# Pairs of row quadrants in one PSUM tile, and a written order for the tensor engine, in a decode-attention and MLP backward kernel

## The chip, the cores and the metric

The kernel runs on one core of a Trainium2 chip. The metric is device time in microseconds, from repeated executions; lower is better. Executions of one kernel here differ by one to two per cent, so each changed version is compared with executions of the kernel before on the same chip in the same rounds. A ratio is the mean time of one kernel's fast runs over that of the other's of the same rounds, so it isn't quite the ratio of the medians that are quoted. A run counts as slow, and is left out of a ratio, when it is over 1.5% above the fastest of its kernel. Spans and shares are from one profiled execution.

PE is the tensor engine (PEld its weight loads), DVE the vector engine, ACT the scalar engine, POOL the engine that issues the output DMAs, SP the queue that issues the loads. PSUM is the memory in which matmuls leave their results; an eviction is the copy of such a tile to SBUF, from where it is stored. A row quadrant is 32 of the 128 rows of PE's array (32*128 in the profile's forms, where the full array is 128*128). The granted clock is the share of its full speed that PE's clock has, by the records of the profile.

## The reference, cut to what matters

One decode step (2 rows, one token each) of attention with a long cache plus a gated MLP, and the gradients of all of it:

```python
B, D, Hq, Hkv, Sk, Dh, F = 2, 576, 32, 16, 4096, 128, 4608     # bf16
def fwd(x, k_cache, v_cache, wq, wo, w_gate, w_up, w_down):
    xn = layernorm(x)
    q = heads(xn @ wq)
    p = softmax(einsum("bhqd,bhkd->bhqk", q, repeat(k_cache)) * Dh ** -0.5)
    o = einsum("bhqk,bhkd->bhqd", p, repeat(v_cache))
    h = (xn @ w_gate) * (xn @ w_up)
    return x + merge(o) @ wo + h @ w_down
out, vjp = jax.vjp(fwd, ...)
return (out, *vjp(grad_out))       # also dk_cache, dv_cache, and every weight's gradient
```

dk_cache and dv_cache are as large as the caches, 92 MB in and 92 MB out in all. Each is a set of outer products: a column of probabilities (or of their gradients) times a row of 128.

## The kernel before: the parts that matter

There are eight iterations: four groups of four kv heads, times two batch rows. In an iteration the four K heads are loaded, transposed on DVE and scored, then there is a softmax, the four V heads are scored for the gradient of the probabilities, and two contracts (probabilities with V, score gradients with K) follow. Outer products (`outs`) and slices of the MLP and projections (`side`) are popped in between by `fill`.

```python
def ps_o():                                    # two buffers of [128, 2 banks, 512] fp32
    return ps.tile([P, 2, 512], FP32, tag="o", bufs=2, name="ps_o")

def head_scores(src, t, b, g, l, s_ps):
    n = nat([P, NCH, Dh], "kv")                # one of 11 buffers
    nc.sync.dma_start(...)                     # 1 MB
    X = xtile(...);  t32(X, n)                 # 32x32 transposes on DVE, one of 2 buffers
    for be in range(4):
        for cq in range(4):
            nc.tensor.matmul(s_ps[:], lhsT=..., rhs=view(X[:], ...))       # 128x128 array, 256 columns
    return n

def unit(A, cq):                               # of outer_units
    o = [ps_o(), ps_o()]
    for h in range(2):
        for aa in range(2):
            a = 2 * A + aa                     # row quadrant of the array, 32 rows
            nc.tensor.matmul(o[aa][:, h, :], lhsT=rows[32 * a:32 * a + 32, P * h:P * (h + 1)],
                             rhs=BD[t][32 * a:32 * a + 32, cq, :], start=True, stop=True)
    for aa in range(2):
        evac(..., o[aa][:]...)                 # to SBUF on ACT or DVE, 1024 columns

for n in range(NIT):
    ...
    for l in range(G):
        K.append(head_scores(kview, 0, b, g, l, s_ps))
        fill(2, per)                           # two outer units and `per` side units
    ...
    pr, pT, ex, rz = softmax(s_ps)
    ...
    for l in range(G):
        V.append(head_scores(vview, 1, b, g, l, dp_ps))
        if l > 0: contract(pT, V[l - 1], o_sb, l - 1)
        fill(2, per)
    ...                                        # end of V, then the contract of K in the same iteration
```

The order in which PE issues is not the written one here. A scheduler at build time reorders the instructions of each engine.

## Time and profile before

| | before |
|---|---|
| two timed runs | 680.32 and 682.2 us, median 681.26 |
| span of the profiled execution | 666.9 us |
| PE busy | 574.7 us, 86% |
| PE idle between its first and last matmul (gaps over 0.06 us) | 72.8 us |
| mean granted PE clock over the span | 0.716 |

How to read it: PE is nearly always occupied, and its clock stands at full or half speed in turn (the trace's 46 clock records are all 1.0 or 0.5, and each but the last lasts a multiple of 3.413 us; mean 0.716). The prediction shows the main lines. The longest waits of PE (what it waited for, microseconds in total, times, longest):

```profile
PE ps_m L488 <- ACT o_sb L491: 11.4, 3, 4.9
PE ps_m L184 <- DVE xn_bf L165: 10.7, 1, 10.7
PE ps_o L512 <- ACT so L93: 7.9, 27, 1.2
PE ps_sc L475 <- DVE negb L540: 7.7, 4, 2.1
```

No group of waits costs PE more than 11.4 us in the whole program: nearly every hand-over has other work behind it.

### The profile page before, as it was taken

The page shows a single profiled execution, that of the slowest core. Times are in us where ns is not written, and L with a number is a line of the kernel's source. Part 1 is how long each engine was busy: PE and PEld are TensorE (multiplying, and loading weights), DVE is VectorE, ACT ScalarE, POOL GpSimd, SP SyncE. Part 2 cuts the span into 40 slices and gives each one's busy share as a digit, 9 for nine tenths or more (in the row PEclk, how much of TensorE's full clock was granted, in tenths as well). Part 3 has the DMA queues.
Part 4 walks back from the last instruction along what each step waited for, and adds up shares of the span by engine and source line. Part 5 has one row for each costly group of instructions (what it writes and reads, how often), then busy time and mean ns, then how long its engine had stood idle before and what let it go on. Part 6 is the DMA issues. An engine that isn't in the chain of part 4 may idle for free.

```text
span 666.9 us, 14489 instructions
## 1 busy us (share of the span) xinstructions
PE 574.7 (86%) x6297; PEld 298.5 (45%) x6297; DVE 360.4 (54%) x499; ACT 330.7 (50%) x445; POOL 129.8 (19%) x252
## 2 busy tenths in 40 slices
PE   1679997897989999897999999899796999989954
PEld 1455553545534445444543454355553345453411
DVE  8686245546594246636484345637287134862245
ACT  0145655283555545374445635456362655645441
POOL 6131201131121121221122221112022111201111
PEclk9998868597886558598776557578597556885555
DMA  8965989559959879749949969829977688834355
GB/s 296 373 234 189 364 325 371 185 178 420 393 201 340 325 246 339 291 154 408 388 163 365 321 249 348 312 83 362 403 280 267 228 295 326 305 133 166 128 197 197
DMA packets 52824, 185.89 MB, mean 279 GB/s; under 512 B 4077, under 2 KB 19065, under 8 KB 44569
## 3 DMA queue, kind: packets, MB, share of 16 engines
q1 hardware_dynamic: 28392, 92.49, 38.4%
q0 software_dynamic: 24368, 92.48, 37.4%
q8 instruction: 49, 0.80, 0.5%
q14 instruction: 15, 0.11, 0.1%
HBM read 92.48 MB, written 92.48 MB: 277 GB/s over the span
## 4 chain that ended last, share of the span: by engine, by line
PE 49%; issue 15%; DMA 10%; ACT 9%; DVE 8%; POOL 1%; ACTq 0%; POOLq 0%; DVEq 0%
PE ps_o L512 16%; PE ps_sc L475 14%; DMA out_dram<-so 10%; ACT so L93 7%; PE ps_m L488 5%; DVE X L102 3%; PE ps_m L497 2%; PE ps_o L379 2%; PE ps_o L345 2%; DVE so L90 1%; PE ps_m L253 1%; PE ps_m L417 1%; DVE Xw L102 1%; PE ps_o L655 1%; DVE stq L90 1%
## 5 line engine op out<-in xcount | busy, mean ns | idle before, releaser
L93 ACT CAST so<-ps_o 128x1024 bf16<-128x1024 f32 x222 | 217.1, 1019 | 174.2 <-PE ps_o L512 116.7
L475 PE MATMUL ps_sc<-X,W 128*128 128x256 bf16 x1024 | 189.7, 328 | 13.2 <-DVE negb L540 7.7
L102 DVE STREAM_TRANSPOSE X<-kv 128x2048 f32<-128x2048 f32 x64 | 147.0, 2299 | 47.0 <-PE ps_sc L475 21.1
L475 PEld LDWEIGHTS <-W 128*128 128x128 bf16 x1024 | 103.9, 113 | 82.8 <-issue 55.2
L512 PE MATMUL ps_o<-BD,pr 32*128 32x512 bf16 x256 | 91.6, 488 | 6.2 <-ACT so L93 4.4
L512 PE MATMUL ps_o<-BD,ds 32*128 32x512 bf16 x256 | 81.7, 487 | 12.0 <-ACT so L93 3.5
L519 POOL DMA_DIRECT2D out_dram<-so x64 | 48.9, 765 | 193.9 <-ACT so L93 91.8
L90 DVE CAST so<-ps_o 128x1024 bf16<-128x1024 f32 x34 | 41.4, 1218 | 49.1 <-PE ps_o L512 43.3
L488 PE MATMUL ps_m<-kv,dsT 128*32 128x128 bf16 x1024 | 29.4, 285 | 11.4 <-ACT o_sb L491 11.4
L93 ACT CAST stw<-ps_o 128x1024 bf16<-128x1024 f32 x33 | 32.6, 1017 | 11.6 <-PE ps_o L345 9.7
L488 PE MATMUL ps_m<-kv,pT 128*32 128x128 bf16 x1024 | 38.2, 257 | 0.1
L488 PEld LDWEIGHTS <-pT 128*32 128x32 bf16 x1024 | 20.3, 107 | 36.1 <-issue 33.5
L488 PEld LDWEIGHTS <-dsT 128*32 128x32 bf16 x1024 | 23.1, 128 | 29.3 <-issue 27.7
L512 PEld LDWEIGHTS <-ds 32*128 32x128 bf16 x256 | 14.7, 96 | 37.3 <-issue 32.0
L497 PEld LDWEIGHTS ps_m<-R,o_sb 128*128 128x128 f32 x128 | 25.7, 281 | 11.0 <-issue 5.7
L93 ACT CAST std<-ps_o 128x576 bf16<-128x576 f32 x33 | 20.7, 640 | 18.8 <-PE ps_o L379 14.4
L497 PE MATMUL ps_m<-R,o_sb 128*128 128x2 f32 x128 | 27.7, 321 | 2.6 <-DVE cr L566 2.6
L512 PEld LDWEIGHTS <-pr 32*128 32x128 bf16 x256 | 15.7, 97 | 25.3 <-issue 16.9
L491 ACT COPY o_sb<-ps_m 128x128 f32<-128x128 f32 x64 | 17.0, 278 | 20.1 <-PE ps_m L488 19.8
L458 ACT CAST bd<-ps_m 128x512 bf16<-128x512 f32 x16 | 9.4, 587 | 30.7 <-PE ps_m L456 30.6
L379 PE MATMUL ps_o<-dyr,hb 32*128 32x288 bf16 x72 | 19.3, 365 | 4.8 <-ACT std L93 4.7
L261 DVE TENSOR_TENSOR accx<-accx,ps_m 128x160 f32<-128x160 f32 x13 | 4.0, 309 | 35.9 <-PE ps_m L258 35.9
(180 smaller groups left out, 578.4 us busy)
## 6 DMA issues: line engine op xcount, KB each, us to landing
out_dram<-so POOLq DMA_DIRECT2D x64, 1024.0 KB, 7.5
kv<-in_A_k_cache_dram SPq DMA_DIRECT2D x32, 1024.0 KB, 8.4
kv<-in_A_v_cache_dram SPq DMA_DIRECT2D x32, 1024.0 KB, 8.8
out_dram<-stw POOLq DMA_DIRECT2D x18, 512.0 KB, 8.1
wd<-in_B_w_down_dram SPq DMA_DIRECT2D x9, 576.0 KB, 8.2
out_dram<-std POOLq DMA_DIRECT2D x9, 576.0 KB, 4.4
wo<-in_A_wo_dram SPq DMA_DIRECT2D x4, 1152.0 KB, 9.4
wgu<-in_B_w_gate_dram SPq DMA_DIRECT2D x9, 512.0 KB, 9.9
```

The lines of the kernel that those rows point to most:

```text
L90: nc.vector.tensor_copy(out=out, in_=in_)
L93: nc.scalar.copy(out, in_)
L102: nc.vector.transpose(out, in_)
L345: nc.tensor.matmul(o[a // 2][:, a % 2, dc * P:(dc + 1) * P], lhsT=xnr[32 * a:32 * a + 32, dc * P:(dc + 1) * P], rhs=hb[32 * a:32 * a + 32, ...
L379: nc.tensor.matmul(o[aa][:, k, 0:HD2], lhsT=hb[32 * a:32 * a + 32, 0, :], rhs=dyr[32 * a:32 * a + 32, k * HD2:(k + 1) * HD2], start=True, ...
L458: nc.scalar.copy(bd[:], bp[:].rearrange("p l d -> p (l d)"))
L475: nc.tensor.matmul(s_ps[:], lhsT=view(W[t][:], 0, P, (be * G + l) * WW + 24 - 8 * cq, [[1, P]]), rhs=view(X[:], 0, P, 2 * cq * Dh + 64 * ( ...
L488: nc.tensor.matmul(o_ps[32 * cq:32 * cq + 32, :], lhsT=rowsT[:, 4 * h + c4, :], rhs=head[:, 8 * c4 + 2 * cq + h, :], start=(h == 0 and c4 ...
L491: nc.scalar.copy(o_sb[:, l, :], o_ps[:])
L497: nc.tensor.matmul(t_ps[:, 2 * l:2 * l + 2], lhsT=o_sb[:, l, :], rhs=R40[:, 2 * l:2 * l + 2], start=True, stop=True)
L512: nc.tensor.matmul(o[aa][:, h, :], lhsT=rows[32 * a:32 * a + 32, P * h:P * (h + 1)], rhs=BD[t][32 * a:32 * a + 32, cq, :], start=True, sto ...
L519: nc.gpsimd.dma_start(oview[b, 2 * A + aa, :, G * g:G * g + G], m["st"][aa][:].rearrange("p l c d -> p l (c d)"))
```

## The change

The intent has two parts. First, an outer product's PSUM tile is given to a pair of row quadrants, one bank each, so its two matmuls run side by side, and a tile that comes free is refilled by one such pair. Second, PE issues everything in the order of the text. That order is written so that half of a head's scores alternates with two pairs. To make it hold, loads and the build of operands move: the loads of a new group's weights, the contract of K (now in the next iteration), and the buffers (kv 11 to 10, staging 4 to 2 plus 2).

```diff
-        def unit(A, cq):
+        def unit(A, cq, h):
-                o = [ps_o(), ps_o()]
-                for h in range(2):
-                    for aa in range(2):
-                        a = 2 * A + aa
-                        nc.tensor.matmul(o[aa][:, h, :], ...)
+                o = ps_o()
                 for aa in range(2):
-                    evac(m["st"][aa]..., o[aa][:]..., 1024)
+                    a = 2 * A + aa
+                    nc.tensor.matmul(o[:, aa, :], ...)
+                evac(m["st"][:, :, :, 2 * cq + h, :], o[:]..., 1024)
  ... the same for the outer products of the MLP and of wq, wo
+    def slot(src, t, b, g, l, s_ps, per, mid=None):
+        n, X = head_load(src, b, g, l)
+        head_scores(X, t, l, s_ps, 0)       # 8 of the 16 score matmuls
+        more(2)                             # two pairs
+        head_scores(X, t, l, s_ps, 1)
+        if mid: mid()                       # a contract
+        more(2)
+        other(per)                          # side units
+        return n
+    chain = ctx.enter_context(tc.manual_schedule(engines={mybir.EngineType.PE}))
  ... in the loop:
-            K.append(head_scores(kview, 0, b, g, l, s_ps))
-            fill(2, per)
+            K.append(slot(kview, 0, b, g, l, s_ps, per, (lambda: end_of_K(*last)) if l == 0 and last else None))
+        if n + 1 < NIT and b == 1:
+            loaded = group_loads(g + 1)     # new wq and wo, while the old ones are held
-            V.append(head_scores(vview, 1, b, g, l, dp_ps))
+            V.append(slot(vview, 1, b, g, l, dp_ps, per, ...))
-        for l in range(G):
-            contract(dsT, K[l], o_sb, l)    # moved into end_of_K of the next iteration
+        last = (st, b, K, dsT)
```

## The prediction

> **What bounds the kernel now.** I read the busy table first, then the costliest groups, then the order of time on PE, the idle time of DVE, and a table by iteration.
>
> ```profile
> PE 574.7 (86%) x6297; PEld 298.5 (45%) x6297; DVE 360.4 (54%) x499; ACT 330.7 (50%) x445; POOL 129.8 (19%) x252
> L93 ACT CAST so<-ps_o 128x1024 bf16<-128x1024 f32 x222 | 217.1, 1019 | 174.2 <-PE ps_o L512 116.7
> L475 PE MATMUL ps_sc<-X,W 128*128 128x256 bf16 x1024 | 189.7, 328 | 13.2 <-DVE negb L540 7.7
> ```
>
> PE is occupied 86% of the span and nothing else is over 54%. The evictions of the outer products (L93) wait for PE 116.7 us, and the scores (L475) hardly wait for anybody. So PE is the engine to shorten, and the question is what its 575 us are made of. The timeline of PE shows two losses:
>
> ```profile
> 356.74 0.60 PE L512 MATMUL ps_o<-BD,pr 32*128 32x512 bf16 x4
> 358.48 0.59 PE L512 MATMUL ps_o<-BD,pr 32*128 32x512 bf16 x2 [0.59 <-ACT so L93]
> ...
> 331.27 0.40 PE L475 MATMUL ps_sc<-X,W 128*128 128x256 bf16 x2
> 331.60 0.41 PE L655 MATMUL ps_o<-dyr,R 32*128 32x288 bf16 x2
> 331.95 0.95 PE L475 MATMUL ps_sc<-X,W 128*128 128x256 bf16 x7
> ```
>
> Four outer products take 0.60 us, and two take 0.59. The four are two pairs from different row quadrants, which run together. The two share a quadrant and run one after the other: each PSUM tile holds one quadrant, so when one tile comes free the scheduler issues its two matmuls alone. The last three lines show PE alternating between the full array (128*128) and row tiles (32*128). From 331.27 to 331.60 are 0.33 us for two score matmuls that take 0.11 each in a run, so a change of tile shape costs about 0.11 us.
>
> The third loss is the clock. By iteration (from one softmax to the next) the view of windows gives:
>
> ```profile
> core 0: us, PE busy (x) PEld busy (x) DVE busy (x) ACT busy (x) POOL busy (x), PEclk, DMA share, GB/s
> 118.20:187.50 69.30, 61.87 (x766) 35.99 (x765) 37.74 (x51) 35.56 (x51) 14.44 (x32) 0.78 0.79 299
> 187.50:270.10 82.60, 78.57 (x764) 36.21 (x763) 45.17 (x58) 45.94 (x60) 14.21 (x25) 0.66 0.82 290
> 581.10:666.90 85.80, 63.66 (x602) 27.98 (x601) 39.34 (x60) 36.24 (x47) 14.07 (x21) 0.56 0.45 165
> ```
>
> Seven iterations lie between 45.0 and 581.1 us, 76.6 us each. The head before the first softmax is 45, the end after the last 86. In the slower iterations the granted clock is lower. DMA is busy 0.8, so loads aren't free either. The idle time of DVE shows where a load already binds:
>
> ```profile
> 144.05 2.31 DVE L102 STREAM_TRANSPOSE X<-kv 128x2048 f32<-128x2048 f32 x1 [6.67 <-DMA kv<-in_A_v_cache_dram]
> DMA to landing us min/median/max: 5.0/8.6/15.0
> ```
>
> The second line is from the view of the tile kv: a head of 1 MB lands 5.0 us after its issue at the least.
>
> [...] The trace's clock is half or full in multiples of 3.413 us. I weighted each matmul's columns by the share of the array that it uses, by window: over 2,900 of such full-array columns the next window is at full clock, under it at half, in 181 of 185 windows. [...]
>
> **The change part by part.** The work is the same (6205 matmuls in both built programs); order and buffers move.
>
> 1. Pairs. I counted the columns that the longest quadrant streams in each stretch of row-tiled matmuls: 263 thousand before, 157 thousand after. 179 of the 512 matmuls of L512 directly follow one of their own quadrant, after none does. A 512-column matmul streams in 0.215 us at full clock (two of them start 0.215 apart), 0.42 ns a column, 0.59 at the mean granted 0.716. 106 thousand columns save 62 us, 7.8 an iteration.
> 2. Changes of tile shape in PE's order: 748 before, 382 after. 366 x 0.11 = 40 us, 5 an iteration.
> 3. Evictions: as many, 227 so-evictions on ACT against 222, the same widths. Nothing saved; ACT still needs 40 us an iteration, under PE.
> 4. Clock. Full-array work is fixed, about 490 thousand columns, 61 thousand an iteration; at 76.6 us (22.4 windows) that is 2,730 a window, just below the threshold. Half a head and two pairs at half clock take 8 x 0.213 + 2 x 0.43 + 2 x 0.11 = 2.8 us for 2,560 columns, 3,100 a window: enough to lift the clock. I take 0.80 instead of 0.716.
>
> PE's own time in an iteration, before: 663 thousand streamed columns / 8 x 0.42 / 0.716 = 48.6, shape changes 10.3, the fp32 ends of contracts (L497, 1.87 us each, two) 3.7, two-column matmuls 2.3: 64.9, so 11.7 us are waits and small matmuls. After: 557 thousand / 8 x 0.42 / 0.80 = 36.5 + 5.3 + 3.7 + 2.3 = 47.8.
>
> 5. Waits that the written order adds. Before, PE did outer products meanwhile. Per iteration: the softmax, three tiny matmuls with DVE and ACT between (0.28, 0.2, 0.16, 0.5 + 0.2 us and hand-overs, sometimes a transpose of 2.3 ahead), 3.5 us; the MLP slice's chain between down and grads (0.42 + 0.4 us and a transpose of 2.5 on DVE), 3; the end of K behind ACT's copies, 1.5; BD, dscores, group front, 1.5; DVE evictions behind transposes, 3: 12.5 us.
> 6. Loads. The kv buffers go from 11 to 10, and K's four heads are held into the next iteration, until its first score head. In the built program, in every second iteration (new wq and wo are held beside the old), the load of V's third head waits for the first's contract, with only two pairs before its scores. It then takes 5.2 to land + 2.3 transpose + 0.4 = 7.9 us, of which PE covers 1. The same for V's fourth (covered 5), the next K's first (4.5), and the second, behind another load (11 against 3.5): 6.9 + 2.9 + 3.4 + 7.5 = 21 us, 10 an iteration.
>
> Sum: 47.8 + 12.5 + 10 + 3 for the small rest = 73.3 against 76.6. Head 47 (the first scores now come after more loads). End: the V half stays, the tail's pairs alternate between ACT and DVE without half-filled tiles; 79 against 86. 47 + 7 x 73.3 + 79 = 639 us in the profile, against 667. The timed runs of before are 1.02 of the profiled one: 651. I lower it to 640, because waits of 5 and 6 partly overlap each other and are counted in full.
>
> **Rivals.**
> - The loads take the place of what PE saves. For it: DMA share 0.8 before, a wait of 6.67 us already there with 11 buffers, and the waits of step 6 in the program. [...] Iterations of 80 to 85 us, 690 to 715.
> - The clock stays up. For it: every stretch of alternating halves is over the threshold[...]. [...] Then streaming is 29 instead of 36.5 and an iteration about 66 us: 590; with smaller waits 575.
> - ACT becomes the bound: 16 pairs in four heads need 4 x 1.02 us a head, PE at full clock about 5.7 with all else. For it 116.7 us of waiting turn round; against, ACT at 40 us an iteration is under any PE estimate. It would cap the gain near 590 too.
> - Saved PE time is hidden anyway: not likely, since PE sits on half of the ending chain.
>
> **Range and chances.** The central sum lies 4 to 6% below before. The added waits are the least certain term (22 us an iteration, perhaps 12 to 32, which is 70 us either way), the clock the next (7 us an iteration, 50 us). Together 80% of outcomes lie between 575 and 700. Faster by over 2% (below 667.6): 0.66. Within: 0.20. Slower: 0.14.
>
> **What would show it.** Right: two outer products of L512 in about 0.38 us at full clock, never 0.59; PE's groups by L512's line busy a third less; ACT's wait for PE on so well below 117; fewer issue gaps at weight loads; granted clock about 0.80. DVE waiting on kv loads grows from 26 us to over 50, mostly in every second iteration at V's third and fourth heads and the next K's second; PE waits on DVE's softmax results rise from about 11 us. Wrong: a clock at or under 0.72 (step 4), kv waits under 30 us (step 6), or PE idle by less than 12 us an iteration (steps 5 and 6 together).

The sum comes to 639 us in the profile, 651 in timed runs, lowered to 640. A window is a stretch of 3.413 us, and the threshold is the 2,900 full-array columns in the trace of before. Steps 5 and 6 assume that in a written order PE does nothing else during a wait. That was not shown when they were written; the runs below measure what the order costs (PE idles 213.4 us with it, 109.6 in a_sched without).

## The result, and the profile after

The changed kernel takes **746.46 us** (two runs, 742.93 and 749.99) against 681.26. The ratio is 1.1018, 95% interval 1.0843 to 1.1193: slower by a tenth. The outputs are correct.

The busy table and the two groups that the prediction started from, after (a group's line gives busy time and mean ns of one, then the idle time of its engine ahead of it and what ended it):

```profile
PE 513.3 (69%) x6297; PEld 287.7 (38%) x6297; DVE 369.7 (49%) x499; ACT 329.6 (44%) x445; POOL 130.1 (17%) x256
L93 ACT CAST so<-ps_o 128x1024 bf16<-128x1024 f32 x227 | 219.7, 1016 | 237.5 <-PE ps_o L520 215.7
L485 PE MATMUL ps_sc<-X,W 128*128 128x256 bf16 x1024 | 213.6, 377 | 68.7 <-DVE X L102 68.7
```

PE is busy 61 us less, and still the span is 81 us longer, because PE stands idle for 213.4 us instead of 72.8. ACT's waiting for PE was to shrink; it nearly doubled. The scores are as many, but take 377 ns each instead of 328, and they now wait 68.7 us for transposed heads.

The table by iteration, from one softmax to the next (columns as in the prediction's table):

```profile
59.30:135.80 76.50, 55.24 (x745) 32.16 (x741) 36.16 (x46) 40.31 (x56) 10.01 (x20) 0.75 0.73 269
135.80:233.90 98.10, 66.75 (x755) 35.22 (x753) 39.61 (x52) 42.00 (x56) 15.54 (x34) 0.62 0.61 223
233.90:314.50 80.60, 60.37 (x773) 35.31 (x771) 42.71 (x53) 40.12 (x55) 13.42 (x25) 0.71 0.81 296
314.50:413.70 99.20, 64.97 (x757) 34.86 (x754) 42.08 (x54) 39.46 (x54) 15.44 (x33) 0.65 0.61 220
669.90:748.20 78.30, 53.50 (x601) 26.94 (x600) 42.37 (x63) 36.46 (x49) 15.39 (x23) 0.61 0.52 188
```

The seven iterations take (669.9 - 59.3) / 7 = 87.2 us on average, against 76.6 before. Every second one takes some 20 us more: it holds the V half of a group's second row and the K half of the next group, with new weights loaded in it. The DMA share is lower there on average (0.61) than in the other iterations of the table (0.73 and 0.81), so these waits don't come of bandwidth alone: loads are issued late. Yet where PE waits the DMA engines are nearly full. The head that PE waits for until 202.30 (below) was issued at 192.71, while a contract still ran, and its transpose starts 7.2 us later, with the DMA share at 0.92 in that stretch. How a wait divides between the two was not measured.

PE's waits, in the same view as above for before:

```profile
PE ps_sc L485 <- DVE X L102: 68.7, 13, 9.0
PE ps_m L320 <- DVE gT L102: 26.8, 8, 4.8
PE ps_m L184 <- DVE xn_bf L165: 13.3, 1, 13.3
PE ps_o L382 <- ACT so L93: 12.2, 21, 0.9
PE ps_m L544 <- DVE mr L542: 11.8, 8, 4.5
PE ps_o L349 <- ACT so L93: 7.7, 11, 1.1
PE ps_m L551 <- ACT ex L549: 6.8, 8, 0.8
```

L485 are the scores, L320 is a middle step of the MLP chain, L544 and L551 are in the softmax. L382 and L349 are outer products of the side units, which stand in a row, two (L382) or eight (L349) matmuls to a tile, with only two tiles. Added over all their lines and releasers, the side units' outer products wait 62 us.

What the waits do to the clock is seen in PE's order of time around the start of a new group's K heads:

```profile
190.34 1.32 PE L485 MATMUL ps_sc<-X,W 128*128 128x256 bf16 x8
191.59 2.08 PE L497 MATMUL ps_m<-kv,dsT 128*32 128x128 bf16 x128
...
195.80 0.40 PE L463 MATMUL ps_m<-ident,dM 128*128 128x128 bf16 x4
202.30 1.86 PE L485 MATMUL ps_sc<-X,W 128*128 128x256 bf16 x8 [6.10 <-DVE X L102]
204.09 1.03 PE L520 MATMUL ps_o<-BD,ds 32*128 32x512 bf16 x4
205.06 1.89 PE L485 MATMUL ps_sc<-X,W 128*128 128x256 bf16 x8
```

and in the table of windows of the same stretch (window, its length, PE busy and count, granted clock, DMA share, GB/s):

```profile
188.00:195.00 7.00, 7.00 (x159) 0.79 0.32 99
195.00:202.00 7.00, 1.20 (x46) 0.70 0.92 321
202.00:209.00 7.00, 6.70 (x64) 0.50 1.01 410
209.00:216.00 7.00, 6.33 (x92) 0.50 0.79 326
```

In this trace the clock follows what PE did just before: the prediction's count (over or under 2,900 full-array columns in a window of 3.413 us) foretells full or half clock in the next window in 194 of 207. From 188 to 195 PE is busy for all 7.00 us; over the following 7 us the granted clock is 0.70 on average, and PE has only 1.20 us of work in them. When the head at last arrives at 202.3, the clock is down to 0.50, and eight scores take 1.86 us (1.32 at 190.34, where the clock changed midway). The full clock falls in the wait and the half clock on the work. The time average of the clock hides this: it is 0.703, near the 0.716 of before.

I therefore cut PE's busy intervals by the records of the granted clock. "Work" is the busy time at full clock plus half of that at half clock; "clock over work" is work over busy time. PE's busy time ahead of the first clock record is left out (11.0 us before, 12.4 after, between 5.5 and 14.6 in the other runs), so differences of some 10 us of work between runs mean little. Idle time is that between the first record and the last matmul.

| | before | after |
|---|---|---|
| PE busy at full / half clock, us | 218.8 / 344.9 | 157.8 / 343.1 |
| work, us of full clock | 391.3 | 329.3 |
| clock over work | 0.694 | 0.657 |
| idle at full clock / half clock, us | 40.6 / 25.3 | 105.0 / 96.9 |
| score matmuls issued at half clock | 39% | 74% |

The change did take 62 us of full-clock work off PE. But 105.0 us of full clock ran out while PE had nothing to do.

### The profile page after: what moved, and what is told of

Read it like the earlier page. It is cut to its first block, busy times and chain, and to the rows that moved or that the text cites. A ratio compares the mean times of both kernels' runs of the same rounds, so it can differ in the third digit from the quotient of the medians.

```text
span 748.2 us, 14452 instructions
## 1 busy us (share of the span) xinstructions
PE 513.3 (69%) x6297; PEld 287.7 (38%) x6297; DVE 369.7 (49%) x499; ACT 329.6 (44%) x445; POOL 130.1 (17%) x256
## 5 line engine op out<-in xcount | busy, mean ns | idle before, releaser
L93 ACT CAST so<-ps_o 128x1024 bf16<-128x1024 f32 x227 | 219.7, 1016 | 237.5 <-PE ps_o L520 215.7
L485 PE MATMUL ps_sc<-X,W 128*128 128x256 bf16 x1024 | 213.6, 377 | 68.7 <-DVE X L102 68.7
L485 PEld LDWEIGHTS <-W 128*128 128x128 bf16 x1024 | 123.6, 129 | 163.6 <-issue 118.6
L520 PE MATMUL ps_o<-BD,ds 32*128 32x512 bf16 x256 | 59.6, 540 | 5.2 <-ACT so L93 2.9
L520 PE MATMUL ps_o<-BD,pr 32*128 32x512 bf16 x256 | 52.7, 492 | 5.5 <-DVE so L90 2.5
L349 PE MATMUL ps_o<-hb,xnr 32*128 32x128 bf16 x288 | 17.0, 249 | 16.0 <-ACT so L93 7.7
L102 DVE STREAM_TRANSPOSE Xw<-wgu 128x2304 f32<-128x2304 f32 x9 | 23.1, 2563 | 9.7 <-PE ps_sc L485 9.7
L468 DVE TENSOR_SCALAR BD<-bd,maskc 128x512 bf16<-128x512 bf16 x64 | 19.3, 365 | 14.8 <-ACT bd L465 14.8
L497 PE MATMUL ps_m<-kv,pT 128*32 128x128 bf16 x1024 | 24.7, 251 | 0.0
L520 PEld LDWEIGHTS <-ds 32*128 32x128 bf16 x256 | 10.1, 101 | 31.3 <-issue 30.9
L497 PE MATMUL ps_m<-kv,dsT 128*32 128x128 bf16 x1024 | 19.4, 238 | 3.8 <-issue 3.8
L382 PE MATMUL ps_o<-dyr,hb 32*128 32x288 bf16 x72 | 11.5, 317 | 14.3 <-ACT so L93 12.2
L349 PEld LDWEIGHTS <-xnr 32*128 32x128 bf16 x288 | 10.9, 104 | 25.9 <-issue 25.5
```

What stands on the lines that cost most here:

```text
L93: nc.scalar.copy(out, in_)
L102: nc.vector.transpose(out, in_)
L349: nc.tensor.matmul(o[:, aa, dc * P:(dc + 1) * P], lhsT=xnr[32 * a:32 * a + 32, dc * P:(dc + 1) * P], rhs=hb[32 * a:32 * a + 32, 1 + w, :], ...
L382: nc.tensor.matmul(o[:, aa, 0:HD2], lhsT=hb[32 * a:32 * a + 32, 0, :], rhs=dyr[32 * a:32 * a + 32, k * HD2:(k + 1) * HD2], start=True, sto ...
L468: nc.vector.tensor_scalar(BD[t][:, c, :], bd[:], maskc[:, c:c + 1], None, op0=ALU.mult)
L485: nc.tensor.matmul(s_ps[:], lhsT=view(W[t][:], 0, P, (be * G + l) * WW + 24 - 8 * cq, [[1, P]]), rhs=view(X[:], 0, P, 2 * cq * Dh + 64 * ( ...
```

## The experiments

The first theory: the pairs save PE time, and the written order loses more, because each wait that is no longer filled costs its own length and lowers the clock for what comes after it. The rivals: the loads and the lost kv buffer make the whole loss (the first rival of the prediction); pairs of quadrants don't pay at all; the halves that alternate are at fault.

Eleven kernels ran. Each ratio is against the kernel before in the same rounds. Differences in us from the changed kernel (746.46) go across rounds, in which the median of the kernel before lay between 672.4 and 681.3; taken by the ratios, the changed kernel comes out 5 to 8 us nearer to the others that are faster, and as much farther from the slower ones (w_reuse 61 us less than it, w_softmax 24, w_both 86, a_sched 121; w_whole 39 more). The sign `+` or `-` in the short diffs is against the kernel that is named.

### Taking the change apart: four runs beside the same runs of the kernel before (median 672.51)

**a_sched**, the changed kernel with the scheduler free for PE:

```diff
-    chain = ctx.enter_context(tc.manual_schedule(engines={mybir.EngineType.PE}))
```

> The changed kernel without the line that fixes PE's order; all tiles, buffers and the order of the text stay. Theory W (the loss is PE waiting at the head of a fixed order): a scheduler fills the waits again, PE idles about as in the kernel before, and the pairs' saving shows: 640 to 680 us. Theory L (the loss is in the loads: ten kv buffers and K's heads held into the next iteration): the waits on kv loads stay, over 60 us by DVE, and the time stays over 715 us. In the built program the tile shape changes 656 times, and 8 matmuls follow one of their own quadrant.

Measured: 619.79 us (614.4 to 621.17), ratio 0.9212 (0.914 to 0.9284), correct, and better than the 640 to 680 that I expected. The one line costs 746 - 620 = 127 us. From its page:

```profile
PE 490.6 (79%) x6297; PEld 284.9 (46%) x6297; DVE 361.3 (58%) x499; ACT 327.4 (53%) x445; POOL 131.6 (21%) x256
L485 PE MATMUL ps_sc<-X,W 128*128 128x256 bf16 x1024 | 186.5, 328 | 34.8 <-DVE X L102 32.8
```

and from its view of DVE's waits:

```profile
DVE X L102 <- DMA kv<-in_A_k_cache_dram: 45.2, 10, 7.5
DVE X L102 <- DMA kv<-in_A_v_cache_dram: 29.2, 9, 7.8
```

The same two waits of DVE in the changed kernel:

```profile
DVE X L102 <- DMA kv<-in_A_k_cache_dram: 33.9, 10, 8.7
DVE X L102 <- DMA kv<-in_A_v_cache_dram: 32.8, 10, 9.7
```

The loads come no earlier with the scheduler free: DVE waits for them 74.4 us here and 66.7 in the changed kernel. PE merely has other work meanwhile, and so scores wait 34.8 us instead of 68.7. The scores take 328 ns again. So late loads alone are not the cause; what they cost depends on whether PE's order is fixed (PE idles 213.4 us with it fixed, 109.6 here).

**b_order**, the kernel before with PE's order fixed as written:

```diff
+    chain = ctx.enter_context(tc.manual_schedule(engines={mybir.EngineType.PE}))
     side = []
```

> The kernel before with PE's order fixed as written and nothing else changed: 11 kv buffers, K's contracts at the end of their own iteration, tiles of one quadrant. The built order changes tile shape 279 times and has no matmul that follows one of its own quadrant in the stretch's longest queue (154 thousand columns), so PE's own work is as short as in the changed kernel. Theory W: slower than before all the same, 730 to 800 us. Theory L: 630 to 690 us.

Measured: 837.46 us (832.55 to 840.29), ratio 1.246 (1.2367 to 1.2552), correct, and slower than the 730 to 800 expected. In its view of PE's waits, one stands out:

```profile
PE ps_o L512 <- ACT so L93: 96.7, 121, 1.1
PE ps_m L538 <- DVE mr L536: 19.7, 8, 3.7
```

Eight outer products stand in a row after each head there, with two PSUM tiles to take them, so PE waits for an eviction 121 times. PE's idle time rises from 73 to 243 us, which is the whole loss of 171 us between the profiled spans (666.9 to 838.5). The work falls to 332.9 us, but the clock over work falls too, to 0.596, so PE is busy as long as ever (572.4 against 574.7).

**b_pairs**, the kernel before, its loop and its free scheduler, with the paired tiles and the changed buffers:

```diff
-        def unit(A, cq):
+        def unit(A, cq, h):
-                o = [ps_o(), ps_o()]
+                o = ps_o()
   ... as in the change; fill() pops two pairs for one old unit; slot(), end_of_K and the written order left out
```

> The kernel before with only the tiles changed to pairs of quadrants (and the buffers that they need: ten kv buffers, two large staging tiles, two for the rest); its own order of the text, the scheduler free. Same-quadrant followers fall from 244 to 7, columns from 263 to 177 thousand, shape changes stay (720). Theory W: the pairs' saving shows, 86 thousand columns at 0.59 ns are 50 us of PE, so 630 to 670 us. Theory L: ten buffers cost it, 690 us or more.

Measured: 633.76 us (624.91 to 639.19). No interval was formed, as two of its four runs were over 1.5% above its fastest. The means of the fast runs give 628.1 / 671.7 = 0.935, and even its slowest run, 639.19, lies under the fastest of the kernel before, 667.24. The work falls from 391.3 to 348.2 us with as many changes of tile shape (720 against 748), and PE still has only 87.5 us of idle. So pairs pay by themselves.

**b_nat10**, the kernel before with 10 kv buffers:

```diff
-    sb.tile(..., tag="nat", bufs=11, ...)
+    sb.tile(..., tag="nat", bufs=10, ...)
```

> The kernel before with ten kv buffers instead of eleven, nothing else. Theory W: within 3% of before, 675 to 700 us. Theory L: one buffer less already costs a good part of the 65 us, 705 us or more.

Measured: 674.88 us, ratio 1.0074 (0.9983 to 1.0165). The lost buffer alone costs nothing that can be told.

### Which waits: four runs in the written order (before: median 675.41)

**w_reuse** takes the load out of the group boundary: a new group uses the old wq and wo tiles again. Its outputs are wrong.

```diff
-            loaded = group_loads(g + 1)
+            loaded = (st["wq"], st["wo"])
```

> The changed kernel, but a new group takes the wq and wo tiles of the first group again instead of loading its own (the results are wrong on purpose). The two kv buffers that the old pair held stay free, so the loads of V's third and fourth heads and of the next K no longer wait for a contract, and 6.5 MB are not read. If step 6 of the prediction is right (21 us a group boundary, 62 in all), about 680 to 700 us, scores wait for their transposes under 30 us instead of 68.7. If the loads only fill time that PE would lose to the written order anyway: over 725 us.

Measured: 677.63 us, ratio 1.011 (0.9986 to 1.0235), 69 us under the changed kernel and no longer to be told from the kernel before. The run takes out the transfers of new weights, the two buffers that they hold and the wait for them all at once, so it doesn't tell these apart. From its page:

```profile
L485 PE MATMUL ps_sc<-X,W 128*128 128x256 bf16 x1024 | 198.2, 357 | 5.0 <-DVE X L102 5.0
```

The scores' wait goes from 68.7 to 5.0 us, but PE's idle falls by only 39 us (213.4 to 174.4), as other waits take part of its place (the one at L463 grows from 6 to 21). Between the profiled spans the gain is 748.2 - 675.4 = 72.8 us. The other 31 us are busy time: 513.3 falls to 482.3, with the work not less (340.1 against 329.3; 346.8 against 341.7 with the time ahead of the records counted at full clock), since the clock over work rises from 0.657 to 0.715.

**w_softmax** puts the two score halves of the first V head between the softmax's three small matmuls:

```diff
-        pr, pT, ex, rz = softmax(s_ps)
+        one()                                 # max, transpose
   ...
+                head_scores(Xv, 1, l, dp_ps, 0)
+                two()                         # max to all rows, exp
+                more(2)
+                head_scores(Xv, 1, l, dp_ps, 1)
+                pr, pT, ex, rz = three()      # sum, divide
```

> The changed kernel in its written order, but the softmax's three small matmuls stand apart: the second behind the first half of V's first head, the third behind the second half. The 19.6 us that PE idles before them should go: 720 to 730 us. If the clock then stays up longer, less; if V's first half now waits for its transpose instead, 740 us or more.

Measured: 717.11 us, ratio 1.067 (1.0576 to 1.0764), 29 us under the changed kernel. Idle falls by 16.0 us and busy time by 14.2, at the same work (330.3).

**w_spread** moves side units and pairs apart, between the halves and around the contract:

```diff
         head_scores(X, t, l, s_ps, 0)
-        more(2)
+        more(1); other(1); more(1)
         head_scores(X, t, l, s_ps, 1)
+        more(1); other(per - 1)
         if mid: mid()
-        more(2); other(per)
+        more(1)
```

> The changed kernel in its written order, with the other work (MLP slice, back units) and the outer products spread between the halves and around the contract instead of in a row at the slot's end. The eviction waits of the side units (62 us of PE idle) and the wait of selA's matmuls for gT (26.8 us) should fall by half or more if they come from standing in a row: 690 to 715 us. If they only move to other matmuls, or the score heads hold their X tile longer and DVE waits more: 735 us or more. Shape changes rise from 382 to 445, 7 us against it.

Measured: 762.85 us, ratio 1.1347 (1.1247 to 1.1447): no gain, rather a loss. The wait in the MLP chain (L320) falls from 26.8 to 10.5 us, but the scores' rises to 81.5, and idle stays at 214.0. A wait was moved to another place, and the clock over work was lower still, 0.626, though PE idles as long. The windows give a likely reason, which no run tested: of the clock windows at half clock in which PE had no wait over 0.1 us, 27 of 43 were followed by full clock here and 43 of 54 in the changed kernel. They hold fewer columns, weighted by the share of the array in use (3,053 against 3,204 on average), as the side units between the halves use less of the array (on the page of the changed kernel L349 and L382 are 32*128).

**w_whole** keeps a head's 16 score matmuls together, then two pairs, a contract where there is one, and two pairs:

```diff
         head_scores(X, t, l, s_ps, 0)
-        more(2)
         head_scores(X, t, l, s_ps, 1)
+        more(2)
         if mid: mid()
         more(2)
```

> The changed kernel in its written order with the heads not halved: 16 score matmuls, then two pairs, contract, two pairs. Shape changes 295 instead of 382 (9 us less), X tiles are free earlier, so the waits of DVE's transposes for scores (70.7 us) fall; but four pairs follow each other with two PSUM tiles, so PE waits for evictions as in the written order of the kernel before (101 us there). If halving is worth what it was made for: 770 to 810 us. If X tiles held for longer cost as much: 735 to 755 us.

Measured: 779.6 us, ratio 1.159 (1.1484 to 1.1695), 33 us over the changed kernel. The two groups of L520 on its page:

```profile
L520 PE MATMUL ps_o<-BD,ds 32*128 32x512 bf16 x256 | 56.5, 479 | 38.9 <-ACT so L93 36.5
L520 PE MATMUL ps_o<-BD,pr 32*128 32x512 bf16 x256 | 50.4, 441 | 19.5 <-ACT so L93 19.2
```

The same two in the changed kernel:

```profile
L520 PE MATMUL ps_o<-BD,ds 32*128 32x512 bf16 x256 | 59.6, 540 | 5.2 <-ACT so L93 2.9
L520 PE MATMUL ps_o<-BD,pr 32*128 32x512 bf16 x256 | 52.7, 492 | 5.5 <-DVE so L90 2.5
```

They wait 58.4 us, against 10.7 in the changed kernel. So the halves that alternate are not at fault, and in this written order they are better than whole heads: with two tiles, a third pair that follows at once waits for an eviction of some 1.02 us.

### Do the waits add up, and is a free scheduler helped by the order? (before: median 672.44)

**w_both** is w_softmax and w_reuse together, wrong as the latter.

> The change with two waits taken out together: the softmax's three small matmuls separated by score halves, and the old group's wq and wo used again (wrong outputs on purpose). Alone they took 29 and 69 us off 746. If waits only add their own idle time, the two together give about 746 - 98 = 648 and the clock stays near 0.74. If idle also costs clock, [...] the two together take more than the sum: under 640, PE idle near 155 us, granted clock 0.77 or more. If the waits overlap each other, so that one takes the other's place, about 665 or more.

Measured: 655.6 us (655.5 to 658.48), ratio 0.9744 (0.9676 to 0.9812), 91 us under the changed kernel where the two alone give 69 + 29 = 98. So they nearly add; my second alternative, more than the sum, is refuted, and the clock stays under the 0.77 it named (0.752). In the profiled spans, 94.5 us go: 57.1 of idle and 34.7 of busy time, at equal work (333.0), plus 2.7 at the start. The clock's part is thus there in each run, but it grows about as the idle falls, not by leaps.

**a_soft** is w_softmax without the line that fixes PE's order.

> The changed kernel with the scheduler free for PE (620 us before) and the softmax's small matmuls separated by score halves in the written order. A free scheduler already fills those waits, so I expect 612 to 625, within 1% of 620. If the written order still guides it, 600 to 610.

Measured: 615.69 us (609.66 to 625.59), ratio 0.9095 (0.9 to 0.9189), correct. Its ratio lies below a_sched's 0.9212, but the intervals overlap and the chips differ, so I don't tell the two apart.

**a_whole** is w_whole without that line.

> The changed kernel with the scheduler free for PE and the 16 score matmuls of a head in one piece instead of two halves with outer products between. If a free scheduler makes halving unnecessary, 615 to 630, as the other variant with a free scheduler and whole heads (634 us, other places for the contracts) suggests. If halving is what makes it better than that one, 632 to 640.

Measured: 618.93 us (606.68 to 631.93). Its runs scatter, and three of the four, the profiled one among them, are over 1.5% above its fastest, so no ratio was formed. That is within the scatter of a_sched's 619.79: with a free scheduler, whether heads are written in halves makes no difference that these runs show.

### All runs in one table

Work and clock over work are computed as above, from each profiled execution; idle is PE's between its first and last matmul.

| | us, median | PE busy | PE idle | work | clock over work | scores at half clock |
|---|---|---|---|---|---|---|
| before | 681.26 | 574.7 | 72.8 | 391.3 | 0.694 | 39% |
| after | 746.46 | 513.3 | 213.4 | 329.3 | 0.657 | 74% |
| a_sched | 619.79 | 490.6 | 109.6 | 355.4 | 0.735 | 40% |
| b_order | 837.46 | 572.4 | 243.3 | 332.9 | 0.596 | 81% |
| b_pairs | 633.76 | 522.7 | 87.5 | 348.2 | 0.679 | 45% |
| b_nat10 | 674.88 | 575.4 | 78.3 | 385.8 | 0.683 | 41% |
| w_reuse (wrong outputs) | 677.63 | 482.3 | 174.4 | 340.1 | 0.715 | 62% |
| w_softmax | 717.11 | 499.1 | 197.4 | 330.3 | 0.679 | 69% |
| w_both (wrong outputs) | 655.6 | 478.6 | 156.3 | 333.0 | 0.716 | 56% |
| w_whole | 779.6 | 523.7 | 233.3 | 329.6 | 0.645 | 83% |
| w_spread | 762.85 | 528.0 | 214.0 | 327.1 | 0.626 | 71% |
| a_soft | 615.69 | 484.7 | 109.6 | 354.8 | 0.755 | 35% |
| a_whole | 618.93 | 492.1 | 106.8 | 355.0 | 0.731 | 46% |

The written order does give PE the least work, about 330 us against 350 with the scheduler free. It changes the tile shape 382 times where a_sched does 656 times, and 274 changes of 0.09 us (the cost at full clock that the next section gives) would be 25 us; the two differ by 26, or by 21 with the time ahead of the records counted at full clock. But it gives PE some 100 us more idle, and nearly half of that at full clock. Idle time alone does not set the clock: b_pairs idles less than a_sched and has the lower clock over work (87.5 us and 0.679 against 109.6 and 0.735).

## Why the prediction was wrong

The prediction expected 639 us in the profile and the span was 748.2, 109 us more. By its own sum (head + 7 iterations + end): the head took 59.3 instead of 47, 12 us; the end 78.3 instead of 79; the seven iterations 87.2 instead of 73.3, 7 x 13.9 = 97 us.

**Step 4, the clock, failed.** The prediction took 0.80 from the argument that half a head and two pairs hold 3,100 columns a window, "enough to lift the clock". That counted a stretch without waits, while steps 5 and 6 of the same sum placed 22.5 us of waits in each iteration. For such a stretch the step was mostly right: of the 54 windows at half clock in which PE had no wait over 0.1 us, 43 were followed by full clock (21 of 80 in the kernel before). But 140 of 205 windows have waits, and only 22 of these were followed by full clock. Cut to the seven iterations (here from the first instruction of one softmax to that of the next, on DVE), PE did 40.7 us of full-clock work in each. The prediction's own terms come to the same: (47.8 + 3) x 0.80 = 40.6. But the clock over that work was 0.662, so it took 61.5 us instead of 50.8. That is 10.7 us an iteration, 75 of the 97 us. The mean clock over time (0.703 over the span) was the wrong quantity as well; the clock while PE works counts. The full-array columns, some 490 thousand, are 61 thousand in an iteration of 25.5 windows, 2,400 a window, well under the 2,900 of the prediction's count. The count itself held: it foretells 194 of 207 windows after, as 181 of 185 before (columns without the weight tell at best 135 of 187 before). It was applied to the wrong schedule, and with little margin: of the 31 windows after with 2,900 to 3,250 columns, 11 were followed by half clock.

**Steps 1 and 2, pairs and changes of shape**, were about right. Together they were to save 102 us at a clock of 0.716, 73 of full-clock work; 62 were saved. Pairs alone saved 43 in b_pairs, whose order has 86 thousand columns fewer; at the rate of step 1 that is 50 x 0.716 = 36. Both agree with the steps as far as the measure of work can tell (some 10 us). From the starts of neighbouring matmuls, the two of a pair start some 4 ns apart, and a change costs 0.09 us at full clock (a score followed by an outer product starts it after 0.202 us, a score followed by a score after 0.111) and 0.13 to 0.165 at half clock, so 0.11 was a fair mean.

**Step 3, evictions unchanged**, was right: 219.7 us of so-evictions on ACT against 217.1.

**Steps 5 and 6, the waits**, were nearly right in sum, partly by luck, as terms too large and too small offset each other. (21 us at each of three boundaries are 9 us an iteration, not the 10 of the sum.) The prediction had 12.5 + 10 = 22.5 us an iteration; PE's idle was 25.4, so 2.9 us more, 20 of the 97 us. By cause, the loads at the group boundaries were foreseen with 62 us; the scores' wait for their heads was 68.7 us, and the run without those loads gained 69, with 39 us less idle. The softmax was smaller (18.6 us in all, 2.3 an iteration, against 3.5), the MLP chain about as told (26.8 us in all, 3.4 against 3). The waits for evictions were undersized: 3 us an iteration for DVE's alone, while side units' outer products wait 62 us in all, 7.8 an iteration, mostly for ACT. What these steps missed is that each wait costs more than itself. With w_reuse, w_softmax and w_both, 39, 16 and 57 us less idle shortened the span by 73, 33 and 94.5 us, that is 1.65 to 2.06 us for each.

**The head** was undersized by 12 us. a_sched, with the scheduler free, has its first softmax at 56.5 us too (before 44.5), so PE's fixed order isn't needed for it. The loads that now precede the first scores are the likely cause, which no run tested.

**The rivals.** The first, loads that take the place of what PE saves, foresaw iterations of 80 to 85 us and 690 to 715 us; it was nearest. It gave no size for what idle does to the clock. Without those loads (w_reuse) the kernel is level with the one before, so in the written order they cost about the whole net loss. But a_sched has them all and is 8% faster than the kernel before: they cost this much only where PE's order is fixed (746.46 us against 619.79), and without them the other waits still take what the pairs save. The second, a clock that stays up, did not come: the changed kernel has 17 waits over 3 us that begin at full clock, and the clock fell in each of them or within 3.413 us behind it (before, in 3 of 3). ACT did not become the bound.

**The signs named in advance**: two outer products of L520 take 0.37 to 0.39 us at full clock as a rule (right), but most run at half clock, at some 0.6 us. DVE's kv waits grew to 66.7 us (over 50, right). L520's busy time is a third less (59.6 + 52.7 against 91.6 + 81.7, right). ACT's wait for so "well below 117" was 215.7 (wrong). Fewer issue gaps at weight loads was wrong too: 118.6 us at the scores' loads against 55.2. The clock at or under 0.72 was named as what would make step 4 wrong, and that is what came.

What stays open: whether thinner windows are why spreading the side units (w_spread) lowered the clock over work further, and how the cost of the loads divides between buffers and bandwidth. A mended written order that is as fast as the free scheduler was not found; w_both, which avoids two of its waits, is still 36 us above a_sched.

## What to carry to other kernels

Keep a change of data layout apart from a change of issue order: here pairs of quadrants in one PSUM tile gave some 6% by themselves (b_pairs) and 8 to 9% with the change's other moves, the scheduler free (a_sched, 619.79 us, and a_soft, 615.69, beat both kernels), and the fixed order took back more than that. Before fixing an engine's order, list every matmul in it whose input comes from another engine or a load, for with the order fixed PE idled 213.4 us here, against 109.6 with the scheduler free. Don't estimate the clock apart from the waits, and weigh it by work: here the clock over work fell from 0.694 to 0.657 when PE's idle rose from 72.8 to 213.4 us. Taking a microsecond of idle out of this written order shortened it by 1.65 to 2.06 us; whether that holds elsewhere is not shown.
